# Idle products inside batch 1's scores, a store on ScalarE's queue, and one subtraction ahead of the maxima

## The chip, the cores and the metric

The kernel runs on one core of a Trainium2 chip. The metric is device time in microseconds (us) of one execution, the median over several runs. A profile of one execution gives a trace: for each engine the start, the length, the source line and the tiles of every instruction, and for each DMA its issue and landing. The engines go by TensorE (PE, with PEld for its weight loads), VectorE (DVE), ScalarE (ACT), GpSimd (POOL) and SyncE (SP, which issues most DMAs). Times in the trace count from the start of the span.

## The reference

Eight batches of eight heads, 576 positions, head size 64. In each head 32 packed queries attend to the sequence, and then the sequence attends to the 32 packed results; a mixture of eight experts follows, where each position goes to one expert.

```python
p_packed = sm_attn(p, k, v)              # softmax attention, 32 packed rows per head
out = sm_attn(q, p_packed, p_packed)     # (8, 8, 576, 64)
x = out.transpose(0, 2, 1, 3).reshape(4608, 512)
logits = x @ w_gate;  e_idx = argmax(logits)
gate_w = softmax(logits)[e_idx];  eom = sigmoid(x @ w_output_gate)
y[mask e] = gate_w * eom[e] * (relu(x[mask e] @ w1[e]) @ w2[e])   # F = 1024
```

## The kernel before

**Work and order.** The kernel goes batch by batch. For batch b, `encode(b)` makes the packed rows: the scores `s1` of the packed queries against k in two halves (`scores`, four banks of PSUM), their maxima (`nm`, `nmx`, L236 to L239), exponentials `a` (L244), transposes `a1T`, and the product with v. `route(b)` makes the second attention's weights `a2T`, as a high part `ah` (cast on ScalarE, L385) and a low part `al` (`a2T - ah`, VectorE, L388), and the gate, whose last step counts which experts the batch still needs (`g_cnt`, L459 to L463, and `keys`, L464, both on VectorE). `weights(b)` loads the likeliest expert's w1 and w2; w2 comes in four quarters `wst`, each split into a high part `w2h` (ScalarE, L504) and a low part `w2l` (`wst - w2h`, L507, on VectorE in batch 0 and on GpSimd for all four quarters of batch 1). `values_up(b)` multiplies packed rows by w1 (`ps_G`, split as `Gh` on ScalarE and `Gl` on VectorE, L76 and L77). `ffn(b)` makes the hidden groups `ps_h` (eight groups `fc`, each six products of `Gh`, `Gl` with `ah`, `al`), their relu `hT` (ScalarE L586, VectorE's low part L589), and the products `ps_o` with w2 (L620) for the tiles of 128 positions; positions 0 to 255 first, then 256 to 575. 576 is four tiles and 64 rows, so tile 4 has only 64 rows (L641). `product_out` makes a tile; in the second half the order is tile 4, tile 2, tile 3.

**Who sets the order.** The program is scheduled by hand: each engine works in the order in which the program emits its instructions, and an engine's instruction waits in place, with all behind it, until its inputs are there and its output's tile or bank is free. `START` and `PLANS` are strings that emit pieces. In `PLANS[b]`, `11:yy` means: after step 11 of `ffn(b)` emit two pieces of `encode(b + 1)`. W and w are `weights` of batch b and b + 1, t and r `route`, G and g `values_up`, d is `store()`, q, k and v fetch, and a digit i is `keep_warm(i)`. For batch 0 the two pieces at step 11 are the maxima of batch 1, the two y at step 12 its exponentials, and the W there is the low part of w2's last quarter.

**Idle products.** `keep_warm(i)` emits `CFG["warm"][i]` products of zeros into a bank that nothing reads. For i over 5 each is 128 by 512 in bf16 (L118). In the start of the kernel, `y` emits both halves of batch 1's scores, `6` the seventh group, then `G` the first of batch 0's `ps_G`.

**Batch 0's last tiles.** Tiles 0 and 1 are copied out of PSUM without their factor, since the gate is not ready, and `store()`, at step 28 (d), scales them on ScalarE (L606) and stores them. Tile 4 (64 rows, step 27) is copied in part by ScalarE (`low`, L645), summed and scaled by VectorE (L646, L647) and stored by SP (L648). Tiles 2 and 3 are scaled out of PSUM by ScalarE (L606). All output tiles share four buffers, `ob`; tile 3's scaling reuses the buffer from which tile 4 is stored. Banks of PSUM come from two rings of four, "f" and "a"; batch 1's scores hold ring "a", idle products of groups 6 to 8 take ring "f".

Of the kernel before, what the change touches and what calls it, by code (L numbers as in the profile page):

```python
# [18 lines left out]

P = 128  # L20
BANK = 512
CFG = dict(raw=6, rq=2, pa=4, w1=2, wst=4, w2=6, a1T=2, at=2, row=2, ht=4, ob=4, last=(4, 2, 3), warm=(28, 17, 5, 2, 2, 8, 6, 2),
           pool=("w1.0", "w1.1", "w1.2", "w1.3", "w2.0", "w2.1", "w2.2", "w2.3", "w3.3", "w4.3", "w5.3", "w6.3", "w7.3",
                 "al0.0.0"))

# [3 lines left out]
START = "kkvvqqkkYYYY1YY2YYY3YY4YYtYYWtttYtWttty6G7GttGtWtvvqqkkvv"  # L29
BESIDE = "8:ry 9:yrr 10:yrrrt 11:yr 12:wrr 13:wrqq 14:rkk 15:r "  # L30
REST = "16:xr 17:x 18:r 19:xvv 20:x 22:x 24:x 25:xxw 26:ww 27:rw 28:r 30:r 31:rxg 32:xg 33:gw 34:ww"
PLANS = ["1:GG 3:GG 5:GG 6:WW 8:WWW 9:tt 10:tWW 11:yy 12:Wyy 13:tt 14:tt 15:yytt 16:tyy 17:ty 19:y 20:y 21:ryyr 22:yyr 23:t "
# [9 lines left out]
def tile_packed_attn_then_moe(ctx, tc, qT, kT, v, pT, w_go, w1, w2, out):  # L42


    nc = tc.nc
    B, _, _, NPAIR, HS = qT.shape
    NG, S = v.shape[1], 2 * HS
# [6 lines left out]
    SF = TF * P  # L54
# [10 lines left out]

    NA = CFG["pa"]

    def bank(name, tag="a"):
        return pool.tile([P, BANK], F32, tag=tag, name=name, bufs=NA if tag == "a" else 8 - NA)
# [9 lines left out]
    def three(a, b):  # L79

        return [(a[i], b[j]) for i in range(len(a)) for j in range(len(b)) if i + j < 2]
# [31 lines left out]
    def keep_warm(i):  # L113

        ps = bank("warm", "a" if i in (1, 5) else "f")
        for _ in range(CFG["warm"][i]):
            if i > 5 or i in (3, 4):
                nc.tensor.matmul(ps.rearrange("p (a n) -> p a n", a=2), idle[:, :P], wide_idle, start=True, stop=True)  # L118
            else:
                nc.tensor.matmul(ps[:NP, :2 * NP], blank[:, :NP], blank[:, :2 * NP], start=True, stop=True)  # L120
# [20 lines left out]
    no_row = float(2 * B * S)  # L141
    key_i = sb.tile([P, B * T * Q * E], I32, tag="hT", name="key_i", bufs=CFG["ht"], **WIDE)
    nc.gpsimd.iota(key_i, pattern=[[1, B * T * Q * E]], base=0, channel_multiplier=0)
# [12 lines left out]
    row = const.tile([P, B, T], F32, name="row")  # L156
# [17 lines left out]
    def eng(what, *at):  # L174
        return nc.gpsimd if what + ".".join(map(str, at)) in CFG["pool"] else nc.vector

# [7 lines left out]
    def fetch(x):  # L184
# [5 lines left out]
        tag = "rq" if x == "q" else "raw"  # L190
        bufs = CFG[tag]
        if x == "v":
# [18 lines left out]
    def pairs(x, b, hf):  # L211

        t = loaded.pop((x, b, hf))
        return [t[:, c] for c in range(NPAIR)]

    def scores(b, stat, mov, nm, tag):

        ps = [bank(f"ps_{nm}", tag)[:, :HS] for _ in range(NG)]
        by_head(ps, stat, mov)
        return ps  # L220

    def encode(b):
# [3 lines left out]
        sm = sb.tile([P, NG, 2], F32, tag="sm", name="sm", bufs=2)  # L226
        rs = sb.tile([P, NG, 1], F32, tag="rs", name="rs", bufs=2)
        s1 = [scores(b, pt, pairs("k", b, 0), "s1", "a" if b else "f")]
        if b == 0:
            keep_warm(5)  # L230
        s1.append(scores(b, pt, pairs("k", b, 1), "s1", "a" if b else "f"))
        yield
        nmx = []
        for hf in range(2):
# [5 lines left out]
            yield  # L240
        a1 = sb.tile([P, NG, 2, HS], F32, tag="row", name="a1", bufs=CFG["row"])
        for g in range(NG):
# [25 lines left out]
        for g in range(NG):  # L268
            vt, at = loaded.pop(("v", b, g)), ats[g]
# [285 lines left out]
    def ffn(b):  # L555
        ah, al = A.pop(b)
        for (t0, t1) in halves:
# [4 lines left out]
            for fc in range(FC):  # L562
# [29 lines left out]
                if not (b == c0 == fc == 0):  # L592
                    yield
            outs = [product_out(b, t_, c0, hs) for t_ in (CFG["last"] if last else range(t0, t1))]
            if b == 0 and not last:
                yield from chain.from_iterable(zip(*outs))
# [5 lines left out]
    def store():  # L602

        while keep:
            b, t_, ob, ps, sc = keep.pop(0)
            nc.scalar.activation(ob, ob if b < 2 and t_ < 2 else ps, AF.Copy, scale=sc)  # L606
            nc.sync.dma_start(out[b * S + t_ * P:b * S + (t_ + 1) * P], ob)

    def product_out(b, t_, c0, hs):
        w2s = W[b][1]  # L610
        r = min(P, S - t_ * P)
        ps = bank("ps_o", "f")
        c = t_ * P - c0
        ob = sb.tile([P, DM], F32, tag="ob", name="ob", bufs=CFG["ob"])
        sc = scm_all[:r, b, t_:t_ + 1]
        if t_ < TF:
            lo = 640 - 2 * P + c
            for fc in range(FC):
                for i, (a, m) in enumerate(three((hs[fc][:, c:c + P], hs[fc][:, lo:lo + P]), w2s[fc])):
                    nc.tensor.matmul(ps, a, m, start=fc == i == 0, stop=fc == FC - 1 and i == 2)  # L620
                if fc % 2 and (fc < FC - 1):
                    yield
            if (b, t_) == (B - 1, CFG["last"][-1]):
                rows = out[b * S + t_ * P:b * S + (t_ + 1) * P]
                for queue, x in ((nc.sync, slice(0, DM // 2)), (nc.scalar, slice(DM // 2, DM))):
                    nc.vector.tensor_scalar_mul(ob[:, x], ps[:, x], sc)
                    queue.dma_start(rows[:, x], ob[:, x])
            else:
                keep.append((b, t_, ob, ps, sc))
                if b > 1 or t_ > 1:  # L630
                    store()
                else:
                    nc.scalar.copy(ob, ps)
        else:
            seq = []
            for fc in range(FC):
                wh, wl = w2s[fc]
                both, one = (hs[fc][:, c:c + 2 * r], wh, 2 * r), (hs[fc][:, c:c + r], wl, r)
                seq += [one, both] if fc == FC - 1 else [both, one]
            for i, (a, m, n) in enumerate(seq):  # L640
                nc.tensor.matmul(ps[:n], a, m, start=i == 0, stop=i == len(seq) - 1)  # L641
                if i % 6 == 5:
                    yield
            low = sb.tile([r, DM], F32, tag="ob", name="low", bufs=CFG["ob"])
            nc.scalar.copy(low, ps[r:2 * r])  # L645
            nc.vector.tensor_tensor(ob[:r], ps[:r], low, ALU.add)  # L646
            nc.vector.tensor_scalar_mul(ob[:r], ob[:r], sc)  # L647
            nc.sync.dma_start(out[b * S + SF:(b + 1) * S], ob[:r])  # L648
        yield

    def leftover(nb=B, m=P):
# [179 lines left out]
    def place(plan, b):  # L831

        kinds = dict(x=(encode, 2), y=(encode, 1), Y=(encode, 0), r=(route, 1), t=(route, 0), w=(weights, 1), W=(weights, 0),
                     g=(values_up, 1), G=(values_up, 0), l=(first_leftover, 0))
        for c in plan:
            if c in kinds:
                piece(kinds[c][0], b + kinds[c][1])
            elif c == "d":
                store()
            elif c.isdigit():  # L840
                keep_warm(int(c))
            else:
                fetch(c)
# [4 lines left out]
    for b in range(B):  # L848
        plan = {}
        for x in PLANS[b].split():  # L850
            i, what = x.split(":")
# [60 lines left out]
```

## Time and profile before

| | |
|---|---|
| median of 3 runs | 406.87 us (405.43 to 407.37) |
| the profiled execution | 406.96 us, its span 405.3 us |
| TensorE busy | 396.7 us (98% of the span) |
| VectorE, ScalarE, GpSimd busy | 278.7, 181.7, 40.8 us |
| chain that ended last | 84% TensorE, 6% DMA, 6% VectorE, 2% ScalarE |
| DMA | 83.61 MB, mean 206 GB/s |

The busy time of TensorE counts products that overlap each other and whose ends are modelled, so a wait of up to some 0.2 us can be hidden in it. In the rows below an engine's line gives its start, its length, the engine, the source line, the operation, what it writes and reads, the shapes, and how many are merged; in brackets stand how long the engine was idle before it and what ended that.

### The profile page before, as it was taken

To read this page: it belongs to the slowest core of one execution; us is meant where nothing else is said; L and a number is where in the kernel's file an instruction comes from. 1 tells how busy PE (TensorE), PEld (TensorE's weight loads), DVE (VectorE), ACT (ScalarE), POOL (GpSimd) and SP (SyncE) were. 2 spreads that over 40 slices of the span, in tenths; PEclk is the share of its full clock that TensorE was granted. 3 is DMA by queue.
4 is the path that set the end of the run, shared out by engine and by line. 5 is a ranking of instruction groups with operands and counts; after the bars stand their busy time and mean duration, and the time that the engine had idled before them with its cause. 6 is when DMAs were issued, how large, how long until landed. Compare 5 with 4: busy or idle time off the path is not lost.

```text
span 405.3 us, 9745 instructions
## 1 busy us (share of the span) xinstructions
PE 396.7 (98%) x3782; PEld 321.0 (79%) x3782; DVE 278.7 (69%) x800; ACT 181.7 (45%) x409; POOL 40.8 (10%) x39
## 2 busy tenths in 40 slices
PE   8799999999999999999999999999999999999995
PEld 7567876779769888787978888788877888798874
DVE  2579689757964976659675886749775795858640
ACT  2357527643466245533736337442645335531300
POOL 7000001520044000110002000020002000020010
PEclk9999999999999999999999999999999999999999
DMA  7899539926990199304991079702961059101921
GB/s 246 312 326 414 197 97 395 392 93 228 378 335 33 44 348 411 150 27 139 376 409 52 2 262 407 281 27 77 349 238 35 27 175 356 41 28 41 371 82 53
DMA packets 36687, 83.61 MB, mean 206 GB/s; under 512 B 3614, under 2 KB 16288, under 8 KB 36640
## 3 DMA queue, kind: packets, MB, share of 16 engines
q1 hardware_dynamic: 36464, 82.85, 55.8%
q8 instruction: 30, 0.49, 0.5%
q10 hardware_dynamic: 144, 0.13, 0.1%
q14 instruction: 17, 0.14, 0.1%
q0 software_dynamic: 32, 0.00, 0.0%
HBM read 67.76 MB, written 15.27 MB: 205 GB/s over the span
## 4 chain that ended last, share of the span: by engine, by line
PE 84%; DMA 6%; DVE 6%; ACT 2%; issue 1%; SPq 0%; DVEq 0%; ACTq 0%
PE ps_o L620 40%; PE ps_h L85 23%; PE ps_o L641 6%; PE ps_G L92 3%; DMA k<-in_kT_dram 3%; PE ps_pp L92 2%; DMA vt<-in_v_dram 2%; PE ps_s2T L92 2%; DMA out_dram<-ob 2%; PE ps_s L92 2%; PE ps_a1T L253 2%; PE ps_lg L400 1%; ACT w2h L504 1%; DVE w2l L507 1%; DVE hT L589 1%; DVE nm L236 1%
## 5 line engine op out<-in xcount | busy, mean ns | idle before, releaser
L620 PE MATMUL ps_o<-w2h,hT 128*128 128x512 f32 x512 | 167.1, 397 | 0.0
L620 PEld LDWEIGHTS ps_o<-w2h,hT 128*128 128x128 f32 x512 | 96.1, 188 | 26.4 <-ACT Gh L76 4.2
L589 DVE SCALAR_TENSOR_TENSOR hT<-ps_h,hT 128x256 fp32r<-128x256 f32 x192 | 60.8, 352 | 59.0 <-ACT hT L586 58.3
L620 PE MATMUL ps_o<-w2l,hT 128*128 128x512 f32 x256 | 100.2, 391 | 0.1
L85 PE MATMUL ps_h<-ah,Gh 128*128 128x320 f32 (+1 forms) x252 | 77.2, 306 | 0.7 <-DVE hT L589 0.6
L85 PE MATMUL ps_h<-ah,Gl 128*128 128x320 f32 (+1 forms) x252 | 74.8, 297 | 0.0
L85 PE MATMUL ps_h<-al,Gh 128*128 128x320 f32 (+1 forms) x252 | 74.6, 296 | 0.0
L586 ACT ACTIVATE hT<-ps_h 128x320 fp32r<-128x320 f32 (+1 forms) x128 | 51.2, 414 | 42.8 <-PE ps_h L85 41.9
L507 POOL TENSOR_TENSOR w2l<-wst,w2h 128x1024 fp32r<-128x1024 f32 x13 | 31.2, 2402 | 302.9 <-ACT w2h L504 272.7
L620 PEld LDWEIGHTS ps_o<-w2l,hT 128*128 128x128 f32 x256 | 48.1, 188 | 10.0 <-DVE w2l L507 1.0
L85 PEld LDWEIGHTS ps_h<-ah,Gh 128*128 128x128 f32 x252 | 47.7, 189 | 4.4 <-DVE hT L589 1.7
L85 PEld LDWEIGHTS ps_h<-al,Gh 128*128 128x128 f32 x252 | 47.8, 190 | 0.2
L85 PEld LDWEIGHTS ps_h<-ah,Gl 128*128 128x128 f32 x252 | 47.7, 189 | 0.1
L606 ACT ACTIVATE ob<-ps_o,scm_all 128x512 f32<-128x512 f32 x27 | 18.6, 687 | 37.1 <-PE ps_o L620 32.6
L504 ACT CAST w2h<-wst 128x1024 fp32r<-128x1024 f32 (+1 forms) x33 | 33.4, 1045 | 3.4 <-PE ps_o L620 3.0
L507 DVE TENSOR_TENSOR w2l<-wst,w2h 128x1024 fp32r<-128x1024 f32 (+1 forms) x20 | 23.2, 1166 | 6.1 <-ACT w2h L504 6.0
L364 ACT ACTIVATE s<-s 128x576 f32<-128x576 f32 (+2 forms) x18 | 11.4, 632 | 33.0 <-DVE s L361 33.0
L641 PE MATMUL ps_o<-w2h,hT 128*128 128x512 f32 x64 | 25.6, 400 | 0.0
L641 PE MATMUL ps_o<-w2l,hT 128*64 128x512 f32 x64 | 23.8, 392 | 0.0
L77 DVE TENSOR_TENSOR Gl<-ps_G,Gh 128x512 fp32r<-128x512 f32 x28 | 17.4, 680 | 7.8 <-ACT Gh L76 7.8
L385 ACT CAST ah<-a2T 128x576 fp32r<-128x576 f32 (+2 forms) x17 | 10.7, 639 | 24.8 <-DVE a2T L377 24.8
L244 ACT ACTIVATE a<-ps_s,nmx 128x288 f32<-128x288 f32 x32 | 15.8, 505 | 10.7 <-DVE nmx L239 10.7
(196 smaller groups left out, 447.2 us busy)
## 6 DMA issues: line engine op xcount, KB each, us to landing
w<-in_w_dram SPq DMA_DIRECT2D x36, 512.0 KB, 5.5
wst<-in_w_dram SPq DMA_DIRECT2D x36, 512.0 KB, 9.0
vt<-in_v_dram SPq DMA_DIRECT2D x16, 640.0 KB, 8.9
k<-in_kT_dram SPq DMA_DIRECT2D x14, 576.0 KB, 10.0
q<-in_qT_dram SPq DMA_DIRECT2D x14, 576.0 KB, 10.0
out_dram<-ob SPq DMA_DIRECT2D x31, 256.0 KB, 3.7
a_d<-a2T SPq DMA_DIRECT2D x16, 320.0 KB, 8.2
k<-in_kT_dram SPq DMA_DIRECT2D x4, 288.0 KB, 4.3
```

The costliest lines, as they stand in the source:

```text
L77: (lo_eng or nc.vector).tensor_tensor(lo, src, f(hi), ALU.subtract)
L85: res = nc.tensor.matmul(dst, a, m, start=j == 0, stop=j == len(seq) - 1)
L92: res = nc.tensor.matmul(dst, a, m, start=j == 0, stop=j == len(seqs[0]) - 1)
L244: nc.scalar.activation(a1[:, g, hf], s1[hf][g], AF.Exp, bias=nmx[g], scale=QK, accum_out=sm[:, g, hf:hf + 1])
L364: nc.scalar.activation(sf[g], sf[g], AF.Exp, scale=QK)
L504: nc.scalar.copy(h, x)
L507: eng("w", b, j).tensor_tensor(l, x, f(h), ALU.subtract)
L586: nc.scalar.activation(hT[:, :n], ps, AF.Relu)
L589: nc.vector.scalar_tensor_tensor(hT[:, d0:d0 + s1 - s0], ps[:, s0:s1], 0.0, f(hT[:, s0:s1]), op0=ALU.max, op1=ALU.subtract)
L606: nc.scalar.activation(ob, ob if b < 2 and t_ < 2 else ps, AF.Copy, scale=sc)
L620: nc.tensor.matmul(ps, a, m, start=fc == i == 0, stop=fc == FC - 1 and i == 2)
L641: nc.tensor.matmul(ps[:n], a, m, start=i == 0, stop=i == len(seq) - 1)
```

## The change

Four edits. The seventh group of idle products goes from six to four, and a ninth, of four, is added. It is emitted in batch 1's `encode`, between the two halves of its scores (batch 0 keeps its own group there). In batch 0's plan the W of step 12 moves to step 11, ahead of the two y. And batch 0's 64-row store is issued by ScalarE in place of SP; the other batches keep SP.

```diff
-CFG = dict(raw=6, rq=2, ..., warm=(28, 17, 5, 2, 2, 8, 6, 2),
+CFG = dict(raw=6, rq=2, ..., warm=(28, 17, 5, 2, 2, 8, 4, 2, 4),
...
-PLANS = ["1:GG 3:GG 5:GG 6:WW 8:WWW 9:tt 10:tWW 11:yy 12:Wyy 13:tt ...
+PLANS = ["1:GG 3:GG 5:GG 6:WW 8:WWW 9:tt 10:tWW 11:Wyy 12:yy 13:tt ...
...
         s1 = [scores(b, pt, pairs("k", b, 0), "s1", "a" if b else "f")]
-        if b == 0:
-            keep_warm(5)
+        if b < 2:
+            keep_warm(8 if b else 5)
         s1.append(scores(b, pt, pairs("k", b, 1), "s1", "a" if b else "f"))
...
             nc.vector.tensor_scalar_mul(ob[:r], ob[:r], sc)
-            nc.sync.dma_start(out[b * S + SF:(b + 1) * S], ob[:r])
+            (nc.sync if b else nc.scalar).dma_start(out[b * S + SF:(b + 1) * S], ob[:r])
```

## Rows read from the trace of the kernel before

**Rows 1.** The view of cores: span and mean granted clock of TensorE.
```profile
core 0: 405.3 us, clock 0.999
```

**Rows 2.** Timeline of TensorE, 17 to 22.4 us.
```profile
19.70 0.72 PE L92 MATMUL ps_s<-k,pt 64*32 64x288 f32 x16 [1.63 <-DMA k<-in_kT_dram]
20.35 1.47 PE L118 MATMUL warm<-blank 128*128 128x512 bf16 x6
21.75 0.66 PE L92 MATMUL ps_G<-w,ppT 64*32 64x256 f32 x16
```

**Rows 3.** Timeline of ScalarE, 17 to 22.4 us.
```profile
17.60 0.29 ACT L347 COPY s2r<-ps_s2T 128x32 f32<-128x32 f32 x2
```

**Rows 4.** Timeline of VectorE, 36 to 42 us: two quarters of w2's low part.
```profile
36.42 1.22 DVE L507 TENSOR_TENSOR w2l<-wst,w2h 128x1024 fp32r<-128x1024 f32 x1
...
39.52 1.21 DVE L507 TENSOR_TENSOR w2l<-wst,w2h 128x1024 fp32r<-128x1024 f32 x1
```

**Rows 5.** Timeline of TensorE, 39 to 41 us: the products with w2's low part.
```profile
39.18 0.39 PE L620 MATMUL ps_o<-w2l,hT 128*128 128x512 f32 x1
...
39.86 0.39 PE L620 MATMUL ps_o<-w2l,hT 128*128 128x512 f32 x1
...
40.79 0.50 PE L620 MATMUL ps_o<-w2l,hT 128*128 128x512 f32 x1
```

**Rows 6.** Timeline of ScalarE, 62.6 to 77 us.
```profile
62.71 0.58 ACT L645 COPY low<-ps_o 64x512 f32<-64x512 f32 x1
63.78 1.34 ACT L606 ACTIVATE ob<-ob,scm_all 128x512 f32<-128x512 f32 x2 [0.48 <-DVE scm_all L452]
66.26 0.69 ACT L606 ACTIVATE ob<-ps_o,scm_all 128x512 f32<-128x512 f32 x1 [1.15 <-DVE ob L646]
...
67.79 1.07 ACT L504 CAST w2h<-wst 128x1024 fp32r<-128x1024 f32 x1
68.74 0.69 ACT L385 CAST ah<-a2T 128x576 fp32r<-128x576 f32 x1
...
74.46 0.69 ACT L606 ACTIVATE ob<-ps_o,scm_all 128x512 f32<-128x512 f32 x1 [3.17 <-DMA out_dram<-ob]
```

**Rows 7.** Timeline of VectorE, 63.5 to 77 us.
```profile
66.20 0.48 DVE L647 TENSOR_SCALAR ob<-ob,scm_all 64x512 f32<-64x512 f32 x1
...
74.23 0.32 DVE L463 TENSOR_TENSOR g_cnt<-g_cnt,g_ne 128x160 f32<-128x160 f32 x1
74.59 0.33 DVE L464 SCALAR_TENSOR_TENSOR keys<-g_cnt,keys 128x160 f32<-128x160 f32 x1
76.40 0.42 DVE L589 SCALAR_TENSOR_TENSOR hT<-ps_h,hT 128x256 fp32r<-128x256 f32 x1 [1.48 <-ACT hT L586]
```

**Rows 8.** Timeline of VectorE, 70.8 to 72.5 us: `al`, one by one.
```profile
70.71 1.25 DVE L388 TENSOR_TENSOR al<-a2T,ah 128x576 fp32r<-128x576 f32 x1
...
71.89 0.74 DVE L388 TENSOR_TENSOR al<-a2T,ah 128x576 fp32r<-128x576 f32 x1
```

**Rows 9.** Timeline of GpSimd, 60 to 126 us.
```profile
68.94 2.41 POOL L507 TENSOR_TENSOR w2l<-wst,w2h 128x1024 fp32r<-128x1024 f32 x1 [45.89 <-ACT w2h L504]
76.16 7.10 POOL L507 TENSOR_TENSOR w2l<-wst,w2h 128x1024 fp32r<-128x1024 f32 x3 [4.81 <-ACT w2h L504]
113.43 2.40 POOL L507 TENSOR_TENSOR w2l<-wst,w2h 128x1024 fp32r<-128x1024 f32 x1 [30.18 <-DMA k<-in_kT_dram]
```

**Rows 10.** Timeline of VectorE, 115 to 115.7 us.
```profile
115.06 0.82 DVE L420 TENSOR_TENSOR oh<-L,g_mx 128x32 f32<-128x32 f32 x1
```

**Rows 11.** The last tile's two stores, by source line (durations in ns).
```profile
L627 ACTq DMA_DIRECT2D out_dram<-ob x1: 379/379/379, 401.6 to 401.6; - x1
...
DMA to landing us min/median/max: 1.7/1.7/1.8
```

**Rows 12.** Timeline of TensorE, 72.3 to 78.2 us: batch 1's first hidden groups.
```profile
72.61 0.28 PE L85 MATMUL ps_h<-al,Gh 128*128 128x256 f32 x1
...
76.88 0.39 PE L85 MATMUL ps_h<-ah,Gh 128*128 128x256 f32 x1
```

**Rows 13.** TensorE's waits between 60 and 85 us: total us, times, longest.
```profile
PE ps_h L85 <- DVE hT L589: 0.4, 2, 0.2
```

More of the change, by code (lines that the diff above doesn't have):

```diff
@@ L21 @@
 BANK = 512
-CFG = dict(raw=6, rq=2, pa=4, w1=2, wst=4, w2=6, a1T=2, at=2, row=2, ht=4, ob=4, last=(4, 2, 3), warm=(28, 17, 5, 2, 2, 8, 6, 2),
+CFG = dict(raw=6, rq=2, pa=4, w1=2, wst=4, w2=6, a1T=2, at=2, row=2, ht=4, ob=4, last=(4, 2, 3), warm=(28, 17, 5, 2, 2, 8, 4, 2, 4),
            pool=("w1.0", "w1.1", "w1.2", "w1.3", "w2.0", "w2.1", "w2.2", "w2.3", "w3.3", "w4.3", "w5.3", "w6.3", "w7.3",
@@ L31 @@
 REST = "16:xr 17:x 18:r 19:xvv 20:x 22:x 24:x 25:xxw 26:ww 27:rw 28:r 30:r 31:rxg 32:xg 33:gw 34:ww"
-PLANS = ["1:GG 3:GG 5:GG 6:WW 8:WWW 9:tt 10:tWW 11:yy 12:Wyy 13:tt 14:tt 15:yytt 16:tyy 17:ty 19:y 20:y 21:ryyr 22:yyr 23:t "
+PLANS = ["1:GG 3:GG 5:GG 6:WW 8:WWW 9:tt 10:tWW 11:Wyy 12:yy 13:tt 14:tt 15:yytt 16:tyy 17:ty 19:y 20:y 21:ryyr 22:yyr 23:t "
          "24:wt 25:wkkrr 26:rtrr 28:drqq 29:r 31:g 32:gwwr 33:rg 35:ttww",
```

## The prediction

> **What bounds the kernel now.** I read the view of cores first: one core, 405.3 us, TensorE's granted clock 0.999, so the 2.4 GHz level but for the very ends [rows 1]. The profiled execution took 406.96 us, 1.66 us beyond its span and 0.09 us above the median of the runs shown (406.87). TensorE is busy nearly throughout, so the change pays or costs only by what it does to TensorE's order of work, and I went to the three places that it touches: the start [rows 2, 3], the first products with w2 [rows 4, 5], and the passage from batch 0 to batch 1 [rows 6 to 13]. There the reader should look at ScalarE and VectorE. VectorE is behind: it scales the 64 rows 3 us after ScalarE has copied their low half [rows 6, 7]. TensorE's own waits are few, and on them [rows 13].
>
> **Idle products.** TensorE waits 1.63 us before the second half of batch 1's scores, from 18.07 to 19.70, for a DMA of k [rows 2]. Four idle products go there. Six take 1.40 us from their start to that of G's product [rows 2], so 0.23 each and 0.93 for four. They take a bank of the earlier scores, and the last copies out of those end at 17.89 [rows 3]. They lie between 18.07 and 19.0, with 0.7 us to spare, under the DMA: cost 0, or up to 0.9 if the DMA were early. The group after the scores goes from six to four: G starts 2 x 0.23 = 0.45 us earlier, at 21.30. Gain 0.45; bounds 0 (if something else holds G) and 0.47. The granted clock stayed full over the idle 1.63 us, and less of it is idle now, so the clock has no price here.
>
> **Low part of w2 ahead of the maxima.** The subtraction for the last quarter of w2 runs on VectorE from 39.52 to 40.73; the product that needs it starts at 40.79, 0.93 us after the last of its kind, where the one before took 0.68 [rows 4, 5]. Ahead of the maxima it can start when the quarter before is done, at 37.64 [rows 4]; even 0.4 later it ends by 39.3. Gain 0.25. Late next are the maxima, by some 1.6 us, and behind them on ScalarE the exponentials of batch 1. TensorE turns these only after two whole tiles of products, so this cover holds; if it didn't, the gain would go: bounds 0 and 0.25.
>
> **The store on ScalarE's queue.** What goes: ScalarE's last scaling of batch 0 waits 3.17 us, to 74.46, for this store to free its tile [rows 6]. The store stands behind SP's loads, 7.7 us from about 66.7. The nearest row for ScalarE's queue is the kernel's last store: 0.38 us to issue, 1.8 us at most to landing [rows 11]. Any landing within 6 us gives the same sum here, and I take it so.
>
> What comes is a wait. ScalarE works in order, and its issue must wait for VectorE's scaling of the 64 rows, which ends at 66.68 [rows 7]; ScalarE has been done with its copy since 63.29. Queued behind the issue are the scalings of tiles 0 and 1 (at 63.78 before), that of tile 2, the casts of G, of w2's first part, and of a [rows 6]. With 0.38 for the issue tile 0 starts at 67.15. From there it is 1.25 to tile 2 (two scalings, 1.34, less their overlap), and from tile 2's start to the end of w2's cast 2.60 (66.26 to 68.86): 71.00, 2.1 us late. GpSimd's low part follows 0.08 later and takes 2.41 [rows 6, 9]: 71.08 to 73.49.
>
> *First collision.* VectorE's first subtraction for `al` took 1.25 us, the second 0.74: GpSimd was at its low part until 71.35, and the first `al` ended 0.61 after that, at 71.96 [rows 8, 9]. The gate's `oh` shows the same more plainly: 0.82 us for 32 columns, from 115.06 to 115.88, and GpSimd's low part ended at 115.83 [rows 9, 10]. So such an instruction, with both inputs in SBUF, stands still until GpSimd is through. Before, 0.64 us of `al` fell under it. Now `ah`, cast 0.57 after w2's part, is there at 71.57, and `al` stands until 73.49: it ends at 74.10, its second half 0.67 later. TensorE wanted the first at 72.61 [rows 12], the second 0.36 later: it is 74.80 - 72.97 = 1.8 us behind.
>
> *Second collision.* ScalarE's last scaling now starts 2.1 us after 71.29 (where its wait began), less what ScalarE waited in between: near 73.2 in place of 74.46. GpSimd's next low part started 1.70 after it [rows 6, 9]: at 74.9. Three parts took 7.10, so 2.37 each; two fill 74.9 to 79.6, as the second's cast is ready by then. VectorE comes to the gate's `g_cnt` product, both inputs in SBUF, 2.27 us after the first `al` (71.96 to 74.23) [rows 7, 8]: at 76.4, inside. It stands until 77.2. The update of `keys` right behind it also reads twice from SBUF, and GpSimd's next part is queued by then; whichever goes first, one of VectorE's two stands until 79.6. Behind them is the subtraction that frees batch 1's first hidden bank (`hT`): near 80.1 in place of 76.40. TensorE's fourth hidden group follows it, at 80.6 instead of 76.88 [rows 7, 12], 3.7 us late. It gives back its two waits on `hT`, 0.4 us idle [rows 13] and 0.1 of tail at each, 0.6: 3.1 us.
>
> The rows show the standstill for two instructions of one kind (`tensor_tensor`) and none for the `keys` kind (`scalar_tensor_tensor`), so I read them narrowly too: `keys` could pass, which gives 407.3 (first rival). The Trainium skill's "SBUF — State Buffer", section "Who interferes with whom", goes by inputs and not by kinds: a VectorE instruction with two inputs in SBUF and a GpSimd instruction that reads SBUF exclude each other, and the first to issue keeps the shared ports for its whole length. By that rule the sum stays at 409.4; the trace agrees for `al` and `oh`, and no row shows `keys`.
>
> **Sum.** 406.96 - 0.45 - 0.25 + 3.1 = 409.4; on the median, 409.3 us. Its own range is 408.6 (an issue that costs nothing, more given back) to 410.2 (neither gain arrives).
>
> **Rivals.** *One collision only.* `g_cnt` and `keys` both get between two of GpSimd's parts: 1.8 late, 0.7 given back, 0.7 gained before, +0.4: 407.3. For it: they are short (0.32 us). Against: `keys` reads what `g_cnt` writes, so it can't ask for SBUF before that is done, and GpSimd's three parts ran without a gap.
>
> *No collision*, the one on the other side. If `al` starts before GpSimd, or runs beside it, it ends at 72.4 and 73.0, ScalarE's delay is absorbed before TensorE needs it, and the waits on `hT` go: 0.7 here and 0.7 before, 405.5. It decides from the point where the casts of a come ahead of w2's. Against it: w2's cast starts 0.95 us before that of a [rows 6].
>
> *The store lands no sooner*, so that the change doesn't do what it says. Landing 7.7 us after 67.1, it holds the last scaling until 74.9; GpSimd's next part moves to 76.6, right beside `g_cnt` at 76.4, and by who is first the time is 408.6 or 411. For it: the same loads are under way; against: the 1.8 us of the last store, though with no loads beside it. The Trainium skill's "DMA: Bandwidth & Descriptors", section "Issuing engines are not separate DMA queues", speaks for this rival: another issuing engine saves issue time alone, since all queues run on the same DMA engines.
>
> *The clock.* TensorE gets two idle stretches, of about 1.5 and 2.1 us, that could bring it to 1.2 GHz; the 1.63 us before did not. Two us of work at half speed would add 2: 411.
>
> **How the numbers follow.** Both collisions 0.55, one 0.25, none 0.12, late landing 0.05, clock 0.03. The likeliest is 409.3. The range takes both collisions and one whole, and the late landing's lower part: 406.2 to 410.6; "none" lies below it, the clock above. About 0.5%, 2.0 us, is what a measurement tells from no change, so slower begins at 408.9: most of the first case (0.45) and 0.07 of the last two, 0.52. The first's remainder, "one" and most of "none" are the same: 0.44. Faster needs 404.8: 0.04.
>
> **What would show it.** Right: idle products at 18.1 and G near 21.3; ScalarE empty from 63.3 to 66.7; an `al` of nearly 2.5 us that ends 0.6 after GpSimd; a `g_cnt` or `keys` of over 2 us; TensorE idle inside batch 1's first hidden group and before its fourth. Wrong: an `al` under 1 us, `al` ahead of GpSimd, `g_cnt` and `keys` at 0.32, or tile 0 scaled before 66.7.

## The result, and the profile after

The changed kernel takes 410.58 us (median of 6 runs, 409.63 to 411.81) against 406.59 for the kernel before in the same session (6 runs, 405.43 to 407.37): ratio 1.0102, 95% interval 1.0078 to 1.0126, so 4.0 us slower. Forecast were 409.3 and slower. The profiled execution took 411.81 us, the longest of the six, with a span of 410.1. Some 1.3 us of its length come only at 386 us, where TensorE waits 0.8 us for weights (L746, a DMA of `w`); in the other traces that wait is between nothing (store_alone among them) and 0.6 us (low_early), so it varies from execution to execution.

The lines of after that answer to [rows 6]: timeline of ScalarE, 62.5 to 76.5 us.

```profile
62.87 0.58 ACT L645 COPY low<-ps_o 64x512 f32<-64x512 f32 x1
66.87 0.56 ACTq L648 DMA_DIRECT2D out_dram<-ob  x1
67.47 1.34 ACT L606 ACTIVATE ob<-ob,scm_all 128x512 f32<-128x512 f32 x2 [4.03 <-DVE ob L647]
...
70.37 1.07 ACT L504 CAST w2h<-wst 128x1024 fp32r<-128x1024 f32 x1
71.31 1.26 ACT L385 CAST ah<-a2T 128x576 fp32r<-128x576 f32 x2
...
73.42 0.73 ACT L606 ACTIVATE ob<-ps_o,scm_all 128x512 f32<-128x512 f32 x1
```

ScalarE computes nothing from 63.45 to 67.47, held by the issue, which waits for VectorE's L647. What was queued behind it comes late: w2's cast at 70.37 (67.79 before), and the last scaling at 73.42, no longer waiting for a store.

The answers to [rows 9] and to [rows 7, 8]: timelines of GpSimd, 60 to 90 us, and of VectorE, 66 to 80.8 us (the two `al` are merged into one line here).

```profile
71.52 2.37 POOL L507 TENSOR_TENSOR w2l<-wst,w2h 128x1024 fp32r<-128x1024 f32 x1 [46.69 <-ACT w2h L504]
75.15 4.71 POOL L507 TENSOR_TENSOR w2l<-wst,w2h 128x1024 fp32r<-128x1024 f32 x2 [1.26 <-ACT w2h L504]
```

```profile
72.04 3.13 DVE L388 TENSOR_TENSOR al<-a2T,ah 128x576 fp32r<-128x576 f32 x2 [0.72 <-ACT ah L385]
...
76.30 0.31 DVE L459 TENSOR_SCALAR g_cnt<-ps_cnt 128x160 f32<-128x160 f32 x1
76.53 1.04 DVE L461 TENSOR_SCALAR g_ne<-iota,estar_all 128x8 f32<-128x8 f32 x1
77.60 2.44 DVE L463 TENSOR_TENSOR g_cnt<-g_cnt,g_ne 128x160 f32<-128x160 f32 x1
80.08 0.32 DVE L464 SCALAR_TENSOR_TENSOR keys<-g_cnt,keys 128x160 f32<-128x160 f32 x1
80.32 0.75 DVE L589 SCALAR_TENSOR_TENSOR hT<-ps_h,hT 128x256 fp32r<-128x256 f32 x2
```

The reader should lay these two lists beside each other. The first `al` takes 2.46 us of the 3.13 and ends 0.61 after GpSimd (74.50, 73.89). `g_ne`, eight numbers wide, ends at 77.57, when the first of GpSimd's next two parts does (77.54); `g_cnt` ends at 80.04, 0.18 after the second (79.86). Only then can VectorE copy out the hidden bank.

Timeline of TensorE, 72 to 86 us, the answer to [rows 12]; and a window, which gives each engine's busy time (PE, PEld, DVE, ACT, POOL), then the granted clock, 0.50:

```profile
74.56 0.39 PE L85 MATMUL ps_h<-al,Gh 128*128 128x256 f32 x1 [1.75 <-DVE al L388]
...
80.79 0.39 PE L85 MATMUL ps_h<-ah,Gh 128*128 128x256 f32 x1
...
84.56 0.95 PE L253 MATMUL ps_a1T<-ident,a 128*128 128x128 f32 x5
85.66 0.55 PE L253 MATMUL ps_a1T<-ident,a 128*128 128x128 f32 x3 [0.15 <-ACT a L244]
```

```profile
75.04:78.46 3.42, 3.37 (x34) 2.45 (x40) 3.39 (x6) 1.70 (x4) 3.31 (x2) 0.50 1.04 400
```

The product with the first `al` is 1.95 us late (72.61 before) and the fourth hidden group 3.91 (76.88 before), both as forecast within 0.25. After its idle 1.75 us TensorE's granted clock was 0.50 for 3.4 us: the 1.2 GHz level. That is why the wait before the fourth group hardly shows here; the work ahead of it was stretched into it.

The last two lines show a wait that is new. In the trace of before the transposes `ps_a1T` of the next exponentials ran through (timeline of TensorE, 74.2 to 82.6 us):

```profile
81.53 1.13 PE L253 MATMUL ps_a1T<-ident,a 128*128 128x128 f32 x8
```

They begin 3.03 us late, less than the fourth group, since the two waits on `hT` between are gone. Then they stop for ScalarE's exponentials `a`, which start at 83.30 (79.75 before), behind a cast of w2 that is late itself; what follows them starts at 86.05 (82.50 before), 3.55 us late again.

The start and the moved low part, timelines of TensorE, 17 to 22.4 and 39 to 41.5 us, the answers to [rows 2] and [rows 5]:

```profile
18.55 1.04 PE L118 MATMUL warm<-blank 128*128 128x512 bf16 x4
19.52 0.72 PE L92 MATMUL ps_s<-k,pt 64*32 64x288 f32 x16
...
21.72 0.67 PE L92 MATMUL ps_G<-w,ppT 64*32 64x256 f32 x16 [0.52 <-DVE s L376]
...
39.72 0.39 PE L620 MATMUL ps_o<-w2l,hT 128*128 128x512 f32 x1
...
40.41 0.39 PE L620 MATMUL ps_o<-w2l,hT 128*128 128x512 f32 x1
...
41.09 0.39 PE L620 MATMUL ps_o<-w2l,hT 128*128 128x512 f32 x1
```

The idle products lie where they were forecast to, and yet G starts at 21.72, where it started before (21.75). (The profile puts its wait down to VectorE's `s`; the experiments on the start point to a DMA.) The last steps of w2's low part are 0.68 and 0.69, the step of 0.93 is gone.

### The profile page after: what moved, and what is told of

It reads as the page before. It is cut to its first block, busy times and chain, and to the rows that moved or that the text cites. A ratio compares the mean times of both kernels' runs of the same rounds, so it can differ in the third digit from the quotient of the medians.

```text
span 410.1 us, 9748 instructions
## 1 busy us (share of the span) xinstructions
PE 400.1 (98%) x3784; PEld 323.4 (79%) x3784; DVE 282.8 (69%) x800; ACT 181.7 (44%) x409; POOL 40.8 (10%) x39
## 4 chain that ended last, share of the span: by engine, by line
PE 86%; DVE 6%; DMA 3%; ACT 3%; issue 1%; SPq 0%; ACTq 0%; POOL 0%; DVEq 0%
PE ps_o L620 41%; PE ps_h L85 22%; PE ps_o L641 6%; PE ps_G L92 3%; DMA w<-in_w_dram 3%; PE ps_pp L92 2%; PE ps_s2T L92 2%; PE warm L120 2%; PE ps_s L92 2%; PE ps_a1T L253 2%; PE ps_lg L400 1%; ACT a L244 1%; DVE al L388 1%; DVE g_cnt L463 1%; PE ps_lo L746 0%
```

## The experiments

Ratios are to the kernel before, run beside each, with 95% intervals; its medians there were 406.67, 406.54 and 406.79 us. The table compares each trace with the recorded one of before: how much later TensorE starts the same instruction (the difference of the two starts, in us) in the batch before the passage (43 to 45 us), at the product with the first `al`, at the fourth hidden group, and after the passage (84 to 88 us). The last column is after less ahead, what the passage took or gave.

| kernel | ahead | `al` | 4th group | after | passage |
|---|---|---|---|---|---|
| before_again | -0.19 | -0.31 | -0.44 | -0.87 | -0.68 |
| low_early | -0.76 | -0.88 | -1.02 | -1.31 | -0.55 |
| idle_only | +0.13 | +0.01 | -0.12 | -0.38 | -0.51 |
| store_on_sp | +0.19 | +0.06 | -0.07 | -0.28 | -0.47 |
| own_tile | -0.15 | -0.28 | +0.14 | -0.23 | -0.08 |
| own_tile_low1 | -1.38 | -1.51 | -1.64 | -2.09 | -0.71 |
| low_on_vector | +0.02 | +0.68 | +0.96 | +0.52 | +0.50 |
| issue_after_tile2 | -0.16 | +0.94 | +1.21 | +0.75 | +0.91 |
| store_alone | +0.15 | +1.94 | +3.92 | +3.56 | +3.41 |
| the change | +0.15 | +1.94 | +3.91 | +3.57 | +3.42 |
| first_only | -0.19 | +1.61 | +3.95 | +3.59 | +3.78 |
| second_only | -0.99 | -0.34 | +2.76 | +3.22 | +4.21 |

The first four have the passage as it was before, and each takes about 0.55 us less for it than the recorded execution (mean of the four). So that execution was slow there by as much, and what a passage costs is its last column plus 0.55: 3.97 for the change.

**store_alone**: the kernel before with the store's queue alone changed.

```diff
-            nc.sync.dma_start(out[b * S + SF:(b + 1) * S], ob[:r])
+            (nc.sync if b else nc.scalar).dma_start(out[b * S + SF:(b + 1) * S], ob[:r])
```

> The kernel before with the store on ScalarE's queue and nothing else. Theory 1, the collision: the held ScalarE moves GpSimd's low parts onto VectorE's two-input instructions, so the whole loss is in this edit: TensorE 3.0 to 3.6 us late after the passage, 409.6 to 410.2 us against 406.6; al near 2.5 us and one gate instruction near 2.4 us. Theory 2, the start: the idle products and the moved low part cost the larger share of the 4.0 us, and this edit alone gives 407 to 408.5.

410.54 us (409.72 to 412.13), ratio 1.0110 (1.0092 to 1.0127): all of the loss, 0.3 us more than theory 1 had at most. Its stretches of VectorE and GpSimd agree with those of after to 0.02 us. Its waits of TensorE, 60 to 85 us (total, times, longest), and the window of above:

```profile
PE ps_h L85 <- DVE al L388: 1.7, 1, 1.7
PE ps_h L85 <- DVE hT L589: 1.5, 1, 1.5
```

```profile
75.04:78.46 3.42, 3.37 (x63) 2.37 (x62) 3.39 (x6) 1.63 (x4) 3.32 (x2) 1.00 1.04 392
```

Here the clock stayed full, and the second wait, which the slower clock had filled in the profile of after, is plain to see: 1.5 us on the copy out of the bank. The fourth group starts at 80.79 and 80.80. So the clock took no time in that profile; VectorE had set the end already.

**store_on_sp**: the changed kernel with the store back on SP, so idle products and low part alone.

```diff
-            (nc.sync if b else nc.scalar).dma_start(out[b * S + SF:(b + 1) * S], ob[:r])
+            nc.sync.dma_start(out[b * S + SF:(b + 1) * S], ob[:r])
```

> The changed kernel with the store back on SP: idle products and moved low part alone. Theory 1: no standstill at all; as forecast for these two edits 405.9 us (-0.7), or 406.6 if the start is held by the DMA of w1 instead and gives nothing. Theory 2: 408 to 409.5, with a gap of TensorE in the first 46 us.

406.05 us (405.33 to 406.96, 12 runs), ratio 0.9989 (0.9979 to 1.0000). No instruction stands longer than in before (the first `al` 1.26 us, 1.25 there). The two other edits together give about 0.5 us, by the interval 0 to 0.9.

**low_on_vector**: the changed kernel, its first two low parts of batch 1 on VectorE. ScalarE is held as long as before; only what it leads to on GpSimd is taken away.

```diff
-           pool=("w1.0", "w1.1", "w1.2", "w1.3", "w2.0", ...
+           pool=("w1.2", "w1.3", "w2.0", ...
```

> The changed kernel with the first two low parts of batch 1's w2 on VectorE instead of GpSimd; ScalarE is held as long as in the changed kernel. Theory 1: al is 0.75 us again and g_cnt and keys 0.33 us each, TensorE's delay over the passage falls from 3.4 to 0.2 us though VectorE does 2.4 us more: 406.5 to 407.5. Rival, ScalarE's lateness itself (casts 2.2 us late) is the cost and GpSimd only its witness: 409 to 411, no better than the changed kernel.

407.19 us (406.39 to 408.38, 12 runs), ratio 1.0016 (1.0006 to 1.0027). Timeline of VectorE, 70 to 80.8 us:

```profile
71.34 1.23 DVE L507 TENSOR_TENSOR w2l<-wst,w2h 128x1024 fp32r<-128x1024 f32 x1
72.49 1.42 DVE L388 TENSOR_TENSOR al<-a2T,ah 128x576 fp32r<-128x576 f32 x2
...
75.25 0.22 DVE L461 TENSOR_SCALAR g_ne<-iota,estar_all 128x8 f32<-128x8 f32 x1
75.51 0.33 DVE L463 TENSOR_TENSOR g_cnt<-g_cnt,g_ne 128x160 f32<-128x160 f32 x1
75.87 0.33 DVE L464 SCALAR_TENSOR_TENSOR keys<-g_cnt,keys 128x160 f32<-128x160 f32 x1
```

The same `al`, 3.13 us above, takes 1.42; `g_ne` and `g_cnt`, 3.48 together, take 0.55. ScalarE, held for 4.0 us, costs some 1 us of TensorE's time by itself (0.50 + 0.55, with the work that was put on VectorE). The other 3 are the standstills.

**issue_after_tile2**: the changed kernel; ScalarE issues the store only behind tile 2's scaling.

```diff
+            else:
+                late.append((out[b * S + SF:(b + 1) * S], ob[:r]))
...
                     nc.scalar.activation(ob, ob if b < 2 and t_ < 2 else ps, AF.Copy, scale=sc)
                     nc.sync.dma_start(out[b * S + t_ * P:b * S + (t_ + 1) * P], ob)
+                    while late:
+                        nc.scalar.dma_start(*late.pop())
```

> The changed kernel with ScalarE's issue moved behind its scaling of tile 2, so that it waits for VectorE no longer than before. Theory 1: casts 0.5 us later than before, GpSimd's first low part meets only the second al, the next one starts after keys: the passage gains about 0.6 us on the kernel before, 405.5 to 406.5. Rival, a store on ScalarE's queue costs by its issue or its place among the DMAs: 409 or more.

408.06 us (407.12 to 409.19), ratio 1.0046 (1.0030 to 1.0062): a miss, I had thought ScalarE would hardly be held. Timelines of ScalarE, 66 to 76.5, and of VectorE, 70 to 80.8 us:

```profile
67.78 0.56 ACTq L633 DMA_DIRECT2D out_dram<-ob  x1
68.38 1.08 ACT L76 CAST Gh<-ps_G 128x512 fp32r<-128x512 f32 x2 [1.58 <-DVE a2T L377]
...
74.99 0.69 ACT L606 ACTIVATE ob<-ps_o,scm_all 128x512 f32<-128x512 f32 x1 [2.47 <-DMA out_dram<-ob]
```

```profile
71.00 3.16 DVE L388 TENSOR_TENSOR al<-a2T,ah 128x576 fp32r<-128x576 f32 x2 [0.37 <-ACT ah L385]
...
75.77 0.33 DVE L463 TENSOR_TENSOR g_cnt<-g_cnt,g_ne 128x160 f32<-128x160 f32 x1
76.13 0.33 DVE L464 SCALAR_TENSOR_TENSOR keys<-g_cnt,keys 128x160 f32<-128x160 f32 x1
```

The issue comes 1.25 us after VectorE's scaling is done (66.53), and ScalarE stands 1.58 us for it (why it comes so late wasn't settled; the view names `a2T`), and `al` meets GpSimd. But tile 3 now waits for another tile's store, GpSimd's next parts start at 76.69, behind `keys`, and there is no second standstill. This is near the rival of one collision, with ScalarE's 1.58 us on top, and it took 408.06 where the rival's sum gave 407.3.

**second_only** and **first_only**: the changed kernel with one low part alone on VectorE, the first or the second, so that the other standstill is left.

```diff
-           pool=("w1.0", "w1.1", "w1.2", ...
+           pool=("w1.1", "w1.2", ...          # second_only
+           pool=("w1.0", "w1.2", ...          # first_only
```

> The changed kernel with the low part of w2's first quarter of batch 1 on VectorE in place of GpSimd, so that nothing stands in front of al, and the second and third quarters left on GpSimd. Theory (the second standstill sets the end, and what the first costs is absorbed in it): al takes 0.75 and 0.75 us, TensorE waits about 0.6 us for it, but GpSimd still starts its first part near 75.0, so g_ne, g_cnt or keys stand until GpSimd is through, near 79.8, the fourth hidden group starts near 80.4 to 80.8, and the time is 410.0 to 410.7. Rival (the two standstills add up, each with its own price): the time falls by the first one's 1.4 us, to 408.9 to 409.3. Rival (the queue on ScalarE alone costs): as the changed kernel, but with g_cnt and keys at 0.33.

410.68 us (410.49 to 410.77, 4 runs), ratio 1.0093 (1.0071 to 1.0114): no gain from a free `al`. Timeline of VectorE, 70 to 81.2 us, and TensorE's waits, 60 to 85 us:

```profile
71.47 1.42 DVE L388 TENSOR_TENSOR al<-a2T,ah 128x576 fp32r<-128x576 f32 x2
...
74.24 2.19 DVE L461 TENSOR_SCALAR g_ne<-iota,estar_all 128x8 f32<-128x8 f32 x1
76.46 2.42 DVE L463 TENSOR_TENSOR g_cnt<-g_cnt,g_ne 128x160 f32<-128x160 f32 x1
```

```profile
PE ps_h L85 <- DVE hT L589: 2.7, 1, 2.7
PE ps_h L85 <- DVE al L388: 0.6, 1, 0.6
```

The fourth group is 2.76 + 0.99 = 3.75 us later than ahead of the passage, with the change 3.91 - 0.15 = 3.76. The second standstill alone sets the end; the wait on `al` is absorbed in it. In this trace the clock fell after the wait, and here nothing covers it (windows around it):

```profile
79.80:82.90 3.10, 3.10 (x16) 3.10 (x17) 2.66 (x9) 1.69 (x4) 0.29 (x1) 0.50 0.72 300
```

The fourth group is as late as with the change, but the passage ends 0.79 us later (4.21 against 3.42), so here the half clock has a price by the traces. The times don't show it (410.68 and 410.58).

> The changed kernel with the low part of w2's second quarter of batch 1 on VectorE, behind keys, and the first left on GpSimd: al stands as before, 2.4 us, and TensorE waits 1.8 us for it; the second standstill goes, and in its place VectorE has 1.2 us of work ahead of the copy out of the first hidden bank. Theory (the second standstill sets the end): keys done by 77.8, the copy near 79.0 in place of 80.3, the fourth hidden group 1.0 to 1.5 us earlier, 408.3 to 409.3. Rival (the first standstill alone sets the end): no faster than the changed kernel, 410.3 to 410.8. If the third quarter's part on GpSimd, ready near 77.4, meets keys, then up to 410.

410.06 us (408.96 to 410.73, 4 runs), ratio 1.0068 (1.0043 to 1.0092): a miss, a second standstill came back. Timelines of VectorE and GpSimd:

```profile
77.05 3.39 DVE L507 TENSOR_TENSOR w2l<-wst,w2h 128x1024 fp32r<-128x1024 f32 x1
80.36 0.74 DVE L589 SCALAR_TENSOR_TENSOR hT<-ps_h,hT 128x256 fp32r<-128x256 f32 x2
```

```profile
76.83 2.53 POOL L507 TENSOR_TENSOR w2l<-wst,w2h 128x1024 fp32r<-128x1024 f32 x1 [3.27 <-DVE g_cnt L463]
```

The low part that was put on VectorE stands itself, behind GpSimd's part for the third quarter (1.22 when free), and the copy out of the bank starts at 80.36, as with the change.

**own_tile**: the kernel before, the store on SP, but the 64 rows in a buffer outside `ob` (one of the two of `a1T`), so that tile 3's scaling waits for no store: what the store's move was to bring, without ScalarE being held.

```diff
-        ob = sb.tile([P, DM], F32, tag="ob", name="ob", bufs=CFG["ob"])
+        own = b == 0 and t_ == TF
+        ob = sb.tile([P, DM], F32, tag="a1T" if own else "ob", name="ob", bufs=CFG["a1T" if own else "ob"])
```

> The kernel before, its store still on SP, with the 64-row tile in a buffer of its own, so that tile 3's scaling no longer waits 3.17 us for the store. ScalarE is never held. Collision theory: ScalarE comes to batch 1's second high part near 73.2 instead of 75.04, GpSimd's second low part near 74.4 instead of 76.16, on VectorE's keys (74.59) and perhaps g_cnt (74.23); one of them stands to 76.8, or to 79.1 if GpSimd's third part goes first: 406.9 or 409.3 us against 406.67. Rival, the store's wait was a cost and its end is a gain whatever else moves: 405.9 to 406.2.

407.10 us (406.69 to 408.86, 12 runs), ratio 1.0017 (1.0005 to 1.0030): a wait of ScalarE is gone and the kernel is no faster. The wait of 3.17 us had kept GpSimd off VectorE. Tile 3 is now scaled at 72.36 (74.46 before), and GpSimd comes 2 us earlier, in front of `keys` (timelines of VectorE and GpSimd):

```profile
74.18 2.45 DVE L464 SCALAR_TENSOR_TENSOR keys<-g_cnt,keys 128x160 f32<-128x160 f32 x1
```

```profile
74.07 4.82 POOL L507 TENSOR_TENSOR w2l<-wst,w2h 128x1024 fp32r<-128x1024 f32 x2 [3.13 <-ACT w2h L504]
```

**own_tile_low1**: store_on_sp with that buffer, and the second low part on VectorE behind `keys`.

> Idle products and moved low part as in the change, store on SP, the 64-row tile in a buffer of its own, and the second low part of batch 1's w2 on VectorE, behind keys. Collision theory: nothing of GpSimd's falls on a VectorE instruction with two inputs in SBUF but the first al, as before; TensorE's waits on hT go, 0.6 to 0.8 us less than the 406.05 of the version with the store on SP: 405.3 to 405.5. Rival, VectorE's 1.2 us more come on the path: 406.5 to 407.

406.15 us (404.76 to 406.52, 12 runs), ratio 0.9987 (0.9975 to 0.9998). A miss: `keys` takes 0.32 again, but no more than store_on_sp is gained. TensorE's waits, 60 to 85 us:

```profile
PE ps_a1T L253 <- ACT a L244: 0.2, 1, 0.2
```

The waits on `hT` did go: TensorE begins the transposes `ps_a1T` 0.7 us sooner than the first four of the table do (counted from ahead of the passage, 1.31 sooner than the recorded execution; they 0.58 on average). Then it loses 0.60 at the same new wait on `a` that the change met. What was gained is taken back by the next wait.

**idle_only** and **before_again**: the edits at the start alone, and the kernel before once more.

```diff
-    warm=(28, 17, 5, 2, 2, 8, 6, 2)
+    warm=(28, 17, 5, 2, 2, 8, 4, 2, 4)
...
-        if b == 0:
-            keep_warm(5)
+        if b < 2:
+            keep_warm(8 if b else 5)
```

> The changed kernel without the moved low part and with the store on SP: the idle products alone. As forecast, G 0.45 us earlier: 406.2. Rival, G waits for w1's DMA and gains nothing: 406.6, TensorE's wait moved from the k DMA in front of the second half of the scores to the w DMA in front of G.

> The kernel before once more, for another look at its start. If the first loads land some 0.9 us later than in the first profile, as in all profiles since, G's product starts near 21.7 us all the same and w1's DMA lands within 0.3 us of it, so that idle products in front of it cost nothing.

idle_only: 406.71 us (405.75 to 407.99, 12 runs), ratio 0.9997 (0.9983 to 1.0010): no gain seen, though the interval alone would still allow the forecast 0.45. before_again: 406.84 us, one run. Timelines of TensorE, 17 to 25 us, of idle_only and then of before_again:

```profile
18.23 1.04 PE L118 MATMUL warm<-blank 128*128 128x512 bf16 x4
...
21.35 0.73 PE L92 MATMUL ps_G<-w,ppT 64*32 64x256 f32 x16 [0.47 <-DMA w<-in_w_dram]
```

```profile
18.75 0.79 PE L92 MATMUL ps_s<-k,pt 64*32 64x288 f32 x16 [0.32 <-ACT pg L319]
19.48 1.47 PE L118 MATMUL warm<-blank 128*128 128x512 bf16 x6
21.30 0.67 PE L92 MATMUL ps_G<-w,ppT 64*32 64x256 f32 x16 [0.36 <-DMA w<-in_w_dram]
```

With six idle products and with four, G waits for the DMA of w1 and starts at 21.3, so fewer products ahead of it gain nothing. In the profile of the change w1's first part, issued at 18.24, landed 3.3 us later, near 21.5, just ahead of G at 21.72; the `s` named there can't be what G needs, since in before_again G started 0.2 us before that `s` was done (21.09 + 0.42). In this execution of the kernel before, k was no 1.63 us late either: that wait was particular to the execution recorded first.

**low_early**: the kernel before with the low part ahead of the maxima alone.

```diff
-PLANS = ["... 10:tWW 11:yy 12:Wyy ...
+PLANS = ["... 10:tWW 11:Wyy 12:yy ...
```

> The kernel before with one edit: the last low part of w2 ahead of the maxima. The prediction's term: the 0.93 us step between the last two products with w2's low part goes to 0.68, and the gain of 0.25 us stays: ratio 0.9994. Rival (the gain is taken back where the maxima and exponentials are late): the step is 0.68, the ratio 1.0 or above, and a wait of TensorE for the exponentials of batch 1 grows. Rival (this edit gives what the two start edits gave together, 0.5 us): ratio 0.9988.

406.04 us (405.12 to 407.44, 12 runs), ratio 0.9979 (0.9966 to 0.9992). Timeline of TensorE, 39 to 41.5 us:

```profile
39.50 0.39 PE L620 MATMUL ps_o<-w2l,hT 128*128 128x512 f32 x1
...
40.18 0.39 PE L620 MATMUL ps_o<-w2l,hT 128*128 128x512 f32 x1
```

The step is 0.68. In the trace TensorE gains 0.23 there and another 0.15 by 43 us: 0.38 in all, and nothing is lost later. The measured gain, 0.3 to 1.4 us, holds that. This edit alone is the part of the change that pays; alone, with the idle products, or with own_tile_low1's edits, the kernel takes 406.04 to 406.15 us, no two of which these runs tell apart.

## Where the prediction was wrong, and what of it held

The direction was right and the size short: 410.58 lies just inside the range (to 410.6) and beyond the likeliest case's own (to 410.2). As a loss it lies outside: the range stood on 406.87 for the kernel before and so ended 3.7 us above it, while 4.0 us were measured against the kernel before.

**Up to the fourth hidden group the mechanism was the forecast one.** Each step has its line: ScalarE empty until the issue, casts 2.6 us late (forecast 2.1), the first `al` 2.46 us long and done 0.61 after GpSimd, TensorE 1.95 late there (1.8), a `g_cnt` of 2.44, `hT` at 80.32 (80.1), the fourth group at 80.79 (80.6). store_alone puts the whole loss on the store; low_on_vector and second_only show that it is VectorE's standstills, the second above all, and only to a smaller part ScalarE's lateness as such.

**The step that failed is "it gives back its two waits on `hT` ... 0.6: 3.1 us".** The passage took 4.0 us (3.97 in the table's terms), and two things were wrong with the 3.1.

First, the sum ends at the waits on `hT` and puts the wait behind them at nothing. Counted from ahead of the passage, TensorE was 3.76 us late at the fourth group (the sum had 3.7), and 2.88 when it began the transposes `ps_a1T`: the waits on `hT` were given back, and more than 0.6. Then it stood for ScalarE's exponentials, and was 3.40 late behind them: 0.5 of what came back was lost again. own_tile_low1 shows the same wait, with nothing standing but the first `al`. What holds the exponentials was not tested.

Second, the recorded execution was itself slow there. The four other executions of the unchanged passage reach the fourth group 0.25 us sooner and end the passage 0.55 sooner; three have one wait on `hT` left, store_on_sp both. Against those the change is 4.0 late at the fourth group, gets 0.55 back, loses 0.5 to the new wait, and ends 3.97 late. Mis-sized by 0.9. (The issue was too small as well, 0.38 for 0.56; at the fourth group the sum was still only 0.06 short against the recorded execution.)

**The idle products, 0.45 of gain, gave 0.** "Under the DMA: cost 0" held. "G starts 2 x 0.23 = 0.45 us earlier" did not: its lower bound, something else that holds G, was the case, and by idle_only, store_on_sp and before_again it is w1's DMA. I had read one execution's start, in which the lateness of k left the idle products as the last thing ahead of G.

**The moved low part** was 0.25 and gives 0.38 in the traces, since the product after the late one comes sooner too.

With these sizes the sum is 406.6 - 0 - 0.4 + 4.0 = 410.2; the 4.0 us measured (by its interval 3.2 to 5.1) agree with its 3.6.

**Rivals.** One collision: didn't occur here, but issue_after_tile2 came near it, and costs 1.5 by the traces (0.91 + 0.55) and 2.0 by the times (408.06 against store_on_sp's 406.05). No collision: shown false by `al`. *Lands no sooner* was nearly right about the store: it landed 6.3 us after its issue, where it took 7.7 on SP and the sum took "within 6". That is near what the Trainium skill's "DMA: Bandwidth & Descriptors", section "Issuing engines are not separate DMA queues", states, that another issuing engine saves issue time alone. But tile 3's scaling came at 73.42, after the landing near 73.2, so nothing hung on it. The clock: it did fall, in 5 of the 6 runs of after by their mean clock (0.993 to 0.996; 0.999 in the sixth, and 0.997 to 1.000 in the runs of before), but the sixth took 410.74 us and the others 409.63 to 411.81, so that no price shows.

**Which instructions stand.** My doubt about `keys` is settled by own_tile: 2.45 us beside GpSimd. The rule of the Trainium skill's "SBUF — State Buffer", section "Who interferes with whom", which goes by the inputs, agrees with every row here. Its other half I had left out: a `tensor_scalar` with its one input in SBUF can take the shared ports too, if its operands meet certain conditions. `g_ne` did stand, 1.04 and 2.19 us beside GpSimd and 0.22 without; that it stood for this reason is not shown. Not every `tensor_scalar` stands: L459, which reads PSUM, took its 0.31 beside GpSimd at 76.30, and L239 (`nmx`, one number per partition, in SBUF) took 0.21 beside GpSimd in the trace of before (79.50 and 80.11).

## What to carry to other kernels

An issue that waits for another engine holds all that is queued behind it on the issuing engine; before moving one to a busy engine, write down when its input is ready and what starts late behind it. Where VectorE and GpSimd share a stretch, ask of each shift which VectorE instructions will then lie beside GpSimd's: a wait that seems idle may be what keeps them apart, and freeing it (own_tile) can cost. When a sum takes a wait away, look for the wait that comes next on the same engine: own_tile_low1 freed 0.7 us and lost 0.6 of it there. A gain or give-back that rests on a wait seen in one execution should be looked for in a second one before it goes into the sum.

## What the runs showed that I had not expected

- An instruction on 8 numbers per partition (`g_ne`) was held as long as a large one, 2.19 us in second_only, and the next, `g_cnt`, then met GpSimd's following part: two small instructions cost 4.61 us where 0.55 is usual.
- GpSimd stands as well when VectorE is first: in low_on_vector its part, started at 76.25 while VectorE's low part ran (76.11 to 77.33), took 3.35 us in place of 2.4; in own_tile its first, which started together with a VectorE instruction with two inputs in SBUF (L376, 67.93 and 67.94), took 3.00.
- TensorE's granted clock fell to 0.50 after idle stretches of 1.75 us (the change), 1.8 us (first_only) and 2.67 us (second_only), and not in store_alone's trace after 1.7 and 1.5 us. In the change the 3.4 us at half clock cost nothing, since VectorE set the end of that stretch; in second_only they came behind the standstill, and the passage ended 0.79 us later.
